# Attention and routed experts: cast loads, 64-row diagonal products, one copy a pair, 1 MB weight loads

## The chip, the core and the metric

The kernel runs on one NeuronCore of a Trainium2 chip. TensorE (PE) multiplies, VectorE (DVE) and ScalarE (ACT) work on vectors, GpSimd (POOL) works on vectors and issues most of the transfers, SyncE (SP) issues transfers only. The metric is the device time of one execution in microseconds (us); lower is better.

## The reference

```
scores = q @ k^T / 8, for 8 batches x 8 heads, 576 rows of 64
mask:  row block >= column block, blocks of 64 rows
attn   = softmax(scores);  x = attn @ v        -> 4608 rows of 512 (heads side by side)
for e in 0..7:  rows with domain_id == e:  out = relu(x @ w1[e]) @ w2[e]   (512 -> 1024 -> 512)
```

All inputs are float32; the kernel computes in float16 and adds up in float32.

## The kernel before

**Attention** (lines 289 to 471) goes over 32 pairs of heads, four pairs a batch. For pair p it makes: `emit_T`, 36 transposes of q and k as 64x64 tiles into the PSUM tile PT, one half for q and one for k, each copied by DVE to QK (L302); `emit_G` 0 to 2, the scores of key chunks against later queries, and in the last of them 12 products of 64x64 for the diagonal blocks (L336), followed on ACT by exps (L315), four a pair: two of 1024 columns, one of 512, and one of 384 that puts the diagonal blocks into ATE; `emit_P` and `emit_Q`, the products with v into the one PSUM tile `po`: 20 of 65 columns (L366), and 5 of 130 columns that do the diagonal blocks of both heads at once (L361), with ATE zero-padded to 128 rows against VE, a copy of v with the heads in separate row halves. A column of ones beside v gives the softmax sums; `emit_Q` ends with a reciprocal and a multiplication on DVE (L382, L383) into the tile x.

The order is written out by hand (`manual_schedule`): each engine runs its instructions in the order of the code. In the round of pair p, PE gets G0(p), T(p+2), G1(p), P(p-1), G2(p), Q(p-1). Sorting the tokens by domain (`routing`, `inverse`) is cut into steps, one a round, mostly DVE work, some with PE products into PT buffers.

**Loads.** q and k are cast from float32 to float16 by the transfer, issued by POOL, 64 partitions each (L71); two buffers hold two batches each. v comes as float32 into `vst` (three buffers), that of batch 0 on SP's queue (L88), the others on POOL's, one load a head (L104, L108); it is then cast to `vS` by POOL (L114), for batch 0 by DVE. `loads(p)` says in which round POOL issues them. The weights of experts 0 and 1 are loaded in rounds 20 and 22, w1 and w2 in four parts each (L120, L123).

**Experts** (lines 477 on). At the end of each batch the tile x goes to x_rows in device memory. When all has landed, POOL gathers the rows of each expert (L484, five blocks of 128), issues the weights of expert 2, and from then on the weights of expert e+3 between the five scatters of expert e (L540). PE transposes the gathered rows (L494) and does `mm1` (L516) and `mm2` (L533).

Of the kernel before, what the change touches and what calls it, by code (L numbers as in the profile page):

```python
# [18 lines left out]
def kernel(  # L19
# [20 lines left out]
    NH = NJ // 2  # L40

# [25 lines left out]
    def load_qk(g0, g1):  # L67
        t, o = divmod(g0, 2 * HP)
        for src, dst in ((q, qh), (k, kh)):
            for i in range(2):  # L70
                nc.gpsimd.dma_start(  # L71
                    out=dst[t % 2][64 * i : 64 * i + 64, o : o + g1 - g0, :],
                    in_=src.rearrange("b (g i) (p j) d -> i p (b g) (j d)", i=2, j=9)[
                        i, :, g0:g1, :])

    load_qk(0, 1)
# [6 lines left out]

    nc.gpsimd.memset(vst[0][:, :, 0, 0:1], 0.0)
    load_qk(1, HP)
    for c in range(5):
        n = min(128, S - 128 * c)
        nc.sync.dma_start(  # L88
            out=vst[0][0:n, c], in_=v[0, :, 128 * c : 128 * c + n, :].rearrange(
                "h p d -> p h d"))  # L90
    load_qk(HP, 2 * HP)
    up = const.tile([128, 128], F16, name="up")
    make_upper_triangular(nc, up[:], 1.0, diag=False)
    iota_i = const.tile([128, 128], I32, name="iota_i")
    nc.gpsimd.iota(out=iota_i[:], pattern=[[1, 128]], base=0, channel_multiplier=0)
# [6 lines left out]
    def load_v(b, h0, h1):  # L102
        for h in range(h0, h1):
            nc.gpsimd.dma_start(  # L104
                out=vst[b % 3][:, 0:4, h, :],
                in_=v[b, h, 0:512, :].rearrange("(c p) d -> p c d", p=128))
        if h1 == H:
            nc.gpsimd.dma_start(  # L108
                out=vst[b % 3][0:64, 4],
                in_=v[b, :, 512:S, :].rearrange("h p d -> p h d"))  # L110

    def cast_v(fn, b):
        for pr, cs in ((128, slice(0, 2)), (128, slice(2, 4)), (64, slice(4, 5))):
            fn(  # L114
                out=vS[b % 3][0:pr, cs, :, 2:130],
                in_=vst[b % 3][0:pr, cs].rearrange(
                    "p c (g i) d -> p c g (i d)", i=2))

    def w1_piece(w1h, w1_e, i):
        nc.gpsimd.dma_start(out=w1h[:, i], in_=w1_e[128 * i : 128 * i + 128, :])  # L120

    def w2_piece(w2h, w2_e, i):
        nc.gpsimd.dma_start(  # L123
            out=w2h[:, 2 * i : 2 * i + 2],
            in_=w2_e[256 * i : 256 * i + 256, :].rearrange("(p r) f -> p r f", r=2))

    def load_w1(pool, bufs, w1_e):
        w1h = pool.tile([128, 4, Fdim], F16, name="w1h", tag="w1h", bufs=bufs)
        return w1h, [lambda i=i: w1_piece(w1h, w1_e, i) for i in range(4)]

    def load_w2(pool, bufs, w2_e):
        w2h = pool.tile([128, 8, DM], F16, name="w2h", tag="w2h", bufs=bufs)
        return w2h, [lambda i=i: w2_piece(w2h, w2_e, i) for i in range(4)]

    def load_weights(pool, bufs, w1_e, w2_e):
        w1h, t1 = load_w1(pool, bufs, w1_e)
        w2h, t2 = load_w2(pool, bufs, w2_e)
        return w1h, w2h, t1 + t2

    load_v(1, 0, H)  # L140


# [9 lines left out]
    for i in range(3):  # L152
        nc.vector.memset(vS[i][:, :, :, 1:131:129], 1.0)
    for i in range(2):
        nc.vector.memset(ATE[i][:, 0:64], 1.0)
        nc.vector.memset(ATE[i][:, 64:832], 0.0)
        nc.vector.memset(VE[i][:], 0.0)
        nc.vector.memset(VE[i][0:64, :, :, 1:2], 1.0)
        nc.vector.memset(VE[i][64:128, :, :, 130:131], 1.0)
    po = aps.tile([128, 2, 512], F32, name="po")  # L160
    nc.vector.memset(po[:, 1, 264:396], 1.0)

    def inverse(sb, pp, tag, pbufs, ncols, base, tok):
# [5 lines left out]
        for hf in range(2):  # L172
# [7 lines left out]
            nc.vector.tensor_scalar(  # L180
                out=Hh[:, 1], in0=Hh[:, 0], scalar1=p_f[:, 0:1], scalar2=None,
                op0=ALU.mult)
            nc.vector.tensor_tensor(
# [9 lines left out]
            ps = pp.tile([128, 512], F32, name=tag, tag=tag, bufs=pbufs)  # L193
# [40 lines left out]
    def routing():  # L234
        for m in range(0, 128, 32):
            nc.vector.tensor_copy(
                out=iota_x[:, m : m + 32],
                in_=iota_i[:, m : m + 32].unsqueeze(2).to_broadcast([128, 32, NH]))
            yield
        nc.vector.tensor_copy(out=iota_h[:], in_=iota_i[:])  # L240
        nc.vector.tensor_copy(out=p_f[:], in_=p_i[:])
        nc.vector.memset(ones_sq[:], 1.0)
        dom_f = asb.tile([128, NJ], F16, name="dom_f")
        nc.vector.tensor_copy(out=dom_f[:], in_=dom_i[:, 0 : 2 * NJ : 2])
        me = asb.tile([128, E, NJ], F16, name="me")
# [8 lines left out]
        ps_t = aps.tile([128, 512], F32, name="PT", tag="PT", bufs=2)  # L254
        ps_r = aps.tile([128, 512], F32, name="PT", tag="PT", bufs=2)
        nc.tensor.matmul(out=ps_t[:, 0:nj], lhsT=ones_sq[:],
                         rhs=me[:].rearrange(fl), start=True, stop=True)
        nc.tensor.matmul(out=ps_r[:, 0:nj], lhsT=up[:],
# [4 lines left out]
            data1=ps_t[:, 0:nj], initial=0.0, op0=ALU.mult, op1=ALU.add)  # L263
        rk = asb.tile([128, E, NJ], F32, name="rk")
        nc.vector.tensor_tensor(out=rk[:].rearrange(fl), in0=inc[:].rearrange(fl),
                                in1=ps_t[:, 0:nj], op=ALU.subtract)
        nc.vector.tensor_tensor(out=rk[:].rearrange(fl), in0=rk[:].rearrange(fl),
                                in1=ps_r[:, 0:nj], op=ALU.add)
        yield
        nc.vector.tensor_scalar(out=cnt[:], in0=inc[:, :, NJ - 1], scalar1=-1.0,  # L270
                                scalar2=None, op0=ALU.add)
        nc.vector.tensor_tensor(out=rk[:].rearrange(fl), in0=rk[:].rearrange(fl),
                                in1=me[:].rearrange(fl), op=ALU.mult)
        rank = asb.tile([128, NJ], F32, name="rank")
# [3 lines left out]
        ri = slot_col(asb, rank[:], dom_f[:], NJ, u_f[:], "t")  # L278
        lo_i = asb.tile([128, NJ], I32, name="lo_i")
# [3 lines left out]
        yield  # L283
        nc.vector.memset(base_f[:], 0.0)
        yield from inverse(asb, aps, "PT", 2, E * NB, base_f[:, 0:1], tok0[:])

    def emit_T(p):
        b = p // HP  # L290
        QK = asb.tile([128, 2, S], F16, name="QK", tag="QK", bufs=3)
        g = p % (2 * HP)
        for s, src in enumerate((qh[b // 2 % 2], kh[b // 2 % 2])):
            PT = aps.tile([128, 9, 64], F16, name="PT", tag="PT", bufs=2)
            for j in range(9):
                for i in range(2):
                    h = slice(64 * i, 64 * i + 64)
                    nc.tensor.transpose(  # L298
                        out=PT[h, j],
                        in_=src[h, g, 64 * j : 64 * j + 64],  # L300
                        identity=identh[h, h])
            nc.vector.tensor_copy(  # L302
                out=QK[:, s].rearrange("p (n j) -> p n j", j=9),
                in_=PT[:].rearrange("p j n -> p n j"))
        return QK
# [11 lines left out]
    def emit_G(g, st):  # L317
# [11 lines left out]
        else:  # L329
            mm_qk(ps[:, :, 0:256], QK, 2)  # L330
            for m in range(6):
                n0 = 128 * min(m, 4)
                c0 = 256 + 64 * (m % 3)
                for i in range(2):
# [5 lines left out]
            st["A3"] = asb.tile([128, 2, 256], F16, name="A3", tag="A3", bufs=2)  # L340
# [17 lines left out]
    def emit_pv(st, w, m):  # L358
        b, hp = divmod(st["p"], HP)
        o = po[:, w // 3, 132 * (w % 3) : 132 * (w % 3) + 132]  # L360
        nc.tensor.matmul(  # L361
            out=o[:, 1:131], lhsT=st["AE"][:, 128 * m : 128 * m + 128],
            rhs=VE[b % 2][:, m, hp, 1:131], start=True, stop=(m == 0))
        for i in range(2):
            for c in range(m):
                nc.tensor.matmul(  # L366
                    out=o[:, 1 + 65 * i : 66 + 65 * i], lhsT=at_block(st, i, c, m),
                    rhs=vS[b % 3][:, c, hp, 1 + 65 * i : 66 + 65 * i],
                    start=False, stop=(i == 1 and c == m - 1))

    def emit_P(st):
        for m in range(1, 4):
            emit_pv(st, m - 1, m)


    def emit_Q(st):
        hp = st["p"] % HP
# [33 lines left out]
    def loads(p):  # L411
# [8 lines left out]
        if p == 4 * B - 12:  # L420
            w1s[0], t1 = load_w1(wsb, 2, moe_w1[0])
            w2s[0], t2 = load_w2(wsb, 2, moe_w2[0])
            for f in t1:
                f()
# [217 lines left out]
```

## Time and profile before

| | us |
|---|---|
| median of 3 runs | 339.78 (337.0 to 343.36) |
| span of the profiled execution | 337.3 |
| TensorE busy, modelled | 274.4 |
| VectorE, ScalarE, GpSimd busy | 154.0, 140.6, 198.6 |

The profiled execution's own time is not listed apart from its span; the three runs lie between 0.3 below and 6.1 above that span. In the view by stretches a row gives the stretch, its length, the busy time of PE, PEld (weight loads of PE), DVE, ACT and POOL with the number of instructions, then the granted clock of PE as a share of full speed, the busy share of the 16 DMA engines (over 1 where packets overlap) and GB/s as written at the destination. In the timeline a row gives start, length, engine, line and operation; in square brackets the idle time before it and what ended it. In the view of groups a row ends with busy time and mean ns of one.

### The profile page before, as it was taken

The numbers are of one execution on the slowest core, as the hardware profiler recorded it, in microseconds if no ns is written. First come the engines' busy times: TensorE is split into PE (matmuls) and PEld (weight loads), VectorE is DVE, ScalarE is ACT, GpSimd is POOL, SyncE is SP. The second block draws the span as 40 slices with busy tenths as digits, with TensorE's granted clock in tenths as the row PEclk, the third lists the DMA queues.
The fourth block names the chain that finished last, engine by engine and source line by source line (L and its number), as shares of the span: only waits on it lengthen the run. The fifth ranks groups of instructions, "written<-read, shape, count | busy, mean of one in ns | idle before, by whom it ended". The sixth has DMA issues, their size and how long they took to land. (4 is left out here: it accounts for less than half of the span.)

```text
span 337.3 us, 8495 instructions
## 1 busy us (share of the span) xinstructions
PE 274.4 (81%) x3622; PEld 179.6 (53%) x3622; DVE 154.0 (46%) x294; ACT 140.6 (42%) x201; POOL 198.6 (59%) x263
## 2 busy tenths in 40 slices
PE   2404968798989999797169999999999999999930
PEld 1303745566656767575146565665656575656510
DVE  6105896997685688674110433223140504142120
ACT  1211955674753889787015042332405060513200
POOL 8657399556848654000278777768778787523230
PEclk9999995978767899989559999999999999999995
DMA  6999968993899759912337999896989999402020
GB/s 97 205 220 196 221 187 167 218 247 112 153 224 225 150 125 188 220 47 72 84 98 138 251 208 233 166 244 151 211 226 199 233 186 261 157 36 103 32 111 1
DMA packets 36279, 55.66 MB, mean 165 GB/s; under 512 B 9646, under 2 KB 22446, under 8 KB 36240
## 3 DMA queue, kind: packets, MB, share of 16 engines
q0 software_dynamic: 25936, 49.17, 68.2%
q1 hardware_dynamic: 9776, 5.81, 6.6%
q8 instruction: 29, 0.48, 0.5%
q10 hardware_dynamic: 528, 0.13, 0.2%
q14 instruction: 10, 0.08, 0.1%
HBM read 67.15 MB, written 15.20 MB: 244 GB/s over the span
## 5 line engine op out<-in xcount | busy, mean ns | idle before, releaser
L315 ACT ACTIVATE A<-ps 128x1024 f16<-128x1024 f32 (+1 forms) x96 | 83.2, 883 | 64.2 <-PE ps L310 51.1
L522 ACT ACTIVATE hT<-ph 128x640 f16<-128x640 f32 (+1 forms) x72 | 46.4, 645 | 110.0 <-PE ph L516 94.2
L533 PE MATMUL po<-w2h,hT 128*128 128x512 f16 x320 | 74.9, 379 | 0.0
L516 PE MATMUL ph<-xT,w1h 128*128 128x320 f16 x512 | 73.7, 304 | 1.1 <-DVE xT L497 1.1
L484 POOL DMA_INDIRECT xg<-x_rows,tok x40 | 40.6, 1014 | 43.6 <-DMA x_rows<-x 31.6
L540 POOL DMA_INDIRECT out_dram<-osb,tok x40 | 40.8, 1019 | 39.0 <-DVE osb L539 23.7
L516 PEld LDWEIGHTS <-w1h 128*128 128x128 f16 x512 | 50.8, 99 | 23.9 <-issue 1.6
L497 DVE COPY xT<-pt 128x512 f16<-128x512 f16 x40 | 16.8, 424 | 98.9 <-PE pt L494 98.9
L104 POOL DMA_DIRECT2D vst<-in_v_dram x56 | 42.3, 766 | 25.1 <-DMA kh<-in_k_dram 17.9
L302 DVE COPY QK<-PT 128x576 f16<-128x576 f16 x64 | 45.4, 748 | 8.7 <-PE PT L298 8.4
L533 PEld LDWEIGHTS <-hT 128*128 128x128 f16 x320 | 29.8, 98 | 29.4
L310 PE MATMUL ps<-QK 64*128 64x512 f16 (+3 forms) x256 | 38.6, 343 | 1.8 <-DVE QK L302 1.0
L366 PE MATMUL po<-vS,A 128*128 128x65 f16 x640 | 38.5, 205 | 0.8 <-issue 0.8
L361 PE MATMUL po<-VE,ATE 128*128 128x130 f16 x160 | 34.2, 239 | 4.8 <-DVE x L383 2.9
L298 PE MATMUL PT<-identh,qh 64*64 64x64 f16 x576 | 17.5, 208 | 24.7 <-DVE QK L302 16.2
L539 DVE COPY osb<-po 128x512 f32<-128x512 f32 x40 | 27.4, 684 | 18.8 <-PE po L533 18.8
L366 PEld LDWEIGHTS <-A 128*128 128x128 f16 x640 | 33.8, 106 | 3.4 <-issue 3.0
L298 PEld LDWEIGHTS <-qh 64*64 64x64 f16 x576 | 14.2, 121 | 33.4 <-issue 24.3
L383 DVE TENSOR_TENSOR x<-po,rc 128x768 f16<-128x768 f32 x32 | 30.6, 957 | 1.1
L114 POOL CAST vS<-vst 128x1024 f16<-128x1024 f32 (+1 forms) x21 | 18.8, 928 | 9.0 <-PE po L366 6.8
L494 PE MATMUL pt<-identh,xg 128*128 128x128 f16 x160 | 15.8, 226 | 9.1 <-DMA xg<-x_rows,tok 9.1
L361 PEld LDWEIGHTS <-ATE 128*128 128x128 f16 x160 | 16.3, 102 | 10.1 <-issue 8.0
(84 smaller groups left out, 207.7 us busy)
## 6 DMA issues: line engine op xcount, KB each, us to landing
w1h<-in_moe_w_dram POOLq DMA_DIRECT2D x32, 256.0 KB, 6.4
w2h<-in_moe_w_dram POOLq DMA_DIRECT2D x32, 256.0 KB, 7.9
vst<-in_v_dram POOLq DMA_DIRECT2D x63, 128.0 KB, 5.6
x_rows<-x SPq DMA_DIRECT2D x7, 512.0 KB, 4.8
qh<-in_q_dram POOLq DMA_DIRECT2D x6, 576.0 KB, 9.0
kh<-in_k_dram POOLq DMA_DIRECT2D x6, 576.0 KB, 13.2
vst<-in_v_dram SPq DMA_DIRECT2D x4, 256.0 KB, 15.6
xg<-x_rows,tok POOLq DMA_INDIRECT x40, 3.7
```

The source lines that it names most:

```text
L104: nc.gpsimd.dma_start(out=vst[b % 3][:, 0:4, h, :], in_=v[b, h, 0:512, :].rearrange("(c p) d -> p c d", p=128))
L298: nc.tensor.transpose(out=PT[h, j], in_=src[h, g, 64 * j : 64 * j + 64], identity=identh[h, h])
L302: nc.vector.tensor_copy(out=QK[:, s].rearrange("p (n j) -> p n j", j=9), in_=PT[:].rearrange("p j n -> p n j"))
L310: nc.tensor.matmul(out=o[:, i], lhsT=QK[h, 1, 128 * c : 128 * c + 128], rhs=QK[h, 0, 64 + 128 * c : S], start=True, stop=True)
L315: nc.scalar.activation(out=o, in_=i, func=AF.Exp, scale=0.125)
L361: nc.tensor.matmul(out=o[:, 1:131], lhsT=st["AE"][:, 128 * m : 128 * m + 128], rhs=VE[b % 2][:, m, hp, 1:131], start=True, stop=(m == 0))
L366: nc.tensor.matmul(out=o[:, 1 + 65 * i : 66 + 65 * i], lhsT=at_block(st, i, c, m), rhs=vS[b % 3][:, c, hp, 1 + 65 * i : 66 + 65 * i], star ...
L484: nc.gpsimd.indirect_dma_start(out=g[:, blk, :], out_offset=None, in_=xd, in_offset=bass.IndirectOffsetOnAxis(ap=tok[:, 1, blk : blk + 1], ...
L516: nc.tensor.matmul(out=ph[:, i, 0:hw], lhsT=w1_cols(w1h, dc, fc), rhs=xT[:, dc, hw * i : hw * i + hw], start=(dc == 0), stop=(dc == 3))
L522: nc.scalar.activation(out=hT[:, fc].rearrange("p (i n) -> p i n", i=2)[:, i0:i1], in_=ph[:, i0:i1, 0:hw], func=AF.Relu)
L533: nc.tensor.matmul(out=po[:], lhsT=hT[:, fc, 128 * blk : 128 * blk + 128], rhs=w2h[:, fc, :], start=(fc == 0), stop=(fc == 7))
L540: nc.gpsimd.indirect_dma_start(out=dst[blk], out_offset=bass.IndirectOffsetOnAxis(ap=tok[:, 0, blk : blk + 1], axis=0), in_=osb[:], in_off ...
```

## The change

- q and k: one load of 128 partitions for each, four buffers of a batch each. v is cast by the transfer straight into vS, one load a key chunk of 128 rows for all heads (1024 pieces of 64 numbers); vst, POOL's casts and the loads on SP go. Loads of batch b+3 are issued in round 4b.
- The diagonal products with v read the exps in A3 directly, as tiles of 64 rows, 10 of 65 columns (`emit_D`); ATE and VE go, and VB holds the odd heads' v in the upper rows. The exps of 512 and 384 columns become one of 896.
- PT is one buffer for q and k together, copied by one instruction. T(p+2) stands at the end of the round: G0(p), G1(p), P(p-1), G2(p), D(p-1), N(p-1), T(p+2).
- The first routing step stands before the first transposes, the second right behind them; iota_x and four products of `inverse` move to POOL; the sums of `routing` use `po`.
- Weights in four loads an expert, not eight. Expert 0's are issued in round 17; those of experts 1 and 2 after the first gathers.

```diff
-    qh = [asb.tile([128, 2 * HP, S], F16, name=f"qh{i}") for i in range(2)]
-    vst = [asb.tile([128, 5, H, D], F32, name=f"vst{i}") for i in range(3)]
-    vS = [asb.tile([128, 5, HP, 132], F16, name=f"vS{i}") for i in range(3)]
-    VE = [asb.tile([128, 5, HP, 132], F16, name=f"VE{i}") for i in range(2)]
-    ATE = [asb.tile([128, 832], F16, name=f"ATE{i}") for i in range(2)]
+    RV = 4
+    qh = [asb.tile([128, HP, S], F16, name=f"qh{i}") for i in range(RV)]
+    vS = [asb.tile([128, 5, H, 80], F16, name=f"vS{i}") for i in range(RV)]
+    VB = [asb.tile([128, 5, HP, 80], F16, name=f"VB{i}") for i in range(2)]
...
+    def load_v_chunks(b, h0, h1, cs):
+        for c in cs:
+            n = min(128, S - 128 * c)
+            nc.gpsimd.dma_start(
+                out=vS[b % RV][0:n, c, h0:h1, 16:80],
+                in_=v[b, h0:h1, 128 * c : 128 * c + n, :].rearrange("h p d -> p h d"))
...
+    def w1_half(w1h, w1_e, i):
         nc.gpsimd.dma_start(
+            out=w1h[:, 2 * i : 2 * i + 2],
+            in_=w1_e[256 * i : 256 * i + 256, :].rearrange("(c p) f -> p c f", p=128))
...
-            PT = aps.tile([128, 9, 64], F16, name="PT", tag="PT", bufs=2)
+        PT = aps.tile([128, 2, 1024], F16, name="PT", tag="PT", bufs=1)
...
-            emit_exp(st["A3"][:], ps[:, :, 0:256])
-            st["AE"] = ATE[st["p"] % 2]
-            emit_exp(
-                st["AE"][:, 64:832].rearrange(
-                    "p (a m z) -> p a m z", a=2, z=128)[:, :, :, 0:64],
-                ps[:, :, 256:448].rearrange("p a (m z) -> p a m z", z=64))
+            st["A3"] = asb.tile([128, 2, 448], F16, name="A3", tag="A3", bufs=2)
+            emit_exp(st["A3"][:], ps[:, :, 0:448])
...
+    def emit_D(st):
+        b, hp = divmod(st["p"], HP)
+        for m in (1, 2, 3, 4, 0):
+            w = (m - 1) % 5
+            for i in range(2):
+                h = slice(64 * i, 64 * i + 64)
+                n0 = 256 + 64 * (m % 3)
+                r0 = 64 if m else 0
                 nc.tensor.matmul(
+                    out=po[r0:128, i, 65 * w : 65 * w + 65],
+                    lhsT=st["A3"][h, m // 3, n0 - 64 + r0 : n0 + 64],
+                    rhs=(VB[b % 2][h, m, hp, 15:80] if i else
+                         vS[b % RV][h, m, 2 * hp, 15:80]),
+                    start=False, stop=(m == 0))
...
+    def emit_VB(b):
+        nc.vector.tensor_copy(
+            out=VB[b % 2][64:128, :, :, 16:80],
+            in_=vS[b % RV][0:64, :, 1::2, 16:80])
...
+        if p + 2 < npair:
+            QKs[p + 2] = emit_T(p + 2)
+        if p < npair and (p == 0 or hp == HP - 1 and b + 1 < B):
+            emit_VB(0 if p == 0 else b + 1)
+        next(rout, None)
+        if hp == 0 and b + 3 < B:
+            prefetch(b + 3)
+        if p == 4 * (B - 4) + 1:
+            for e in range(1):
+                for f in weights(e):
+                    f()
...
-    w1s[2], w2s[2], todo = load_weights(msb, 4, moe_w1[2], moe_w2[2])
-    for f in todo:
-        f()
+    for e in (1, 2):
+        for f in weights(e):
+            f()
```

How the order moves, at three places. On POOL at the start, before (`DMA` is a transfer issued, destination first; `x2` twice in a row):

```order
L71 DMA qh_69<-in_q_dram 64x3x576 x2
L71 DMA kh_71<-in_k_dram 64x3x576 x2
L71 DMA qh_69<-in_q_dram 64x4x576 x2
L71 DMA kh_71<-in_k_dram 64x4x576 x2
...
L104 DMA vst_74<-in_v_dram 128x4x64 x8
L108 DMA vst_74<-in_v_dram 64x8x64
```

and of the change, from the same place:

```order
L73 DMA vS_77<-in_v_dram 128x4x64 x2
L80 DMA vS_77<-in_v_dram 64x8x64
L68 DMA qh_69<-in_q_dram 128x2x576
L68 DMA kh_73<-in_k_dram 128x2x576
L80 DMA vS_77<-in_v_dram 128x6x64 x4
L68 DMA qh_70<-in_q_dram 128x4x576
```

Batch 0's v (vS_77) now stands on POOL's queue ahead of batch 1's q and k (qh_70); before, POOL issued batch 1's q and k (`64x4x576`) beside batch 0's v, which was on SP's queue.

On DVE in the first rounds, before:

```order
L302 COPY QK<-PT 128x576 x4
L114 CAST vS_76<-vst_73 128x8x128 x2
L114 CAST vS_76<-vst_73 64x4x128
L392 COPY VE_79<-vS_76 64x20x64 x2
L302 COPY QK<-PT 128x576 x4
L382 RECIPROCAL rc<-po 128x12
```

and of the change:

```order
L273 COPY QK<-PT 128x1152
L235 TENSOR_TENSOR rk<-inc,po 128x288
L237 TENSOR_TENSOR rk<-rk,po 128x288
L273 COPY QK<-PT 128x1152 x2
L361 COPY VB_81<-vS_77 64x20x64
L240 CAST p_f<-p_i 128x1
```

The copies for the third pair now stand ahead of the first instruction that waits for v (the copy to VB); before, they stood behind the casts of v.

On POOL where the experts begin, before:

```order
L120 DMA w1h<-in_moe_w_dram 128x1024 x4
L123 DMA w2h<-in_moe_w_dram 128x1024 x4
L484 DMA xg<-x_rows,tok_135 128x512 x10
L120 DMA w1h<-in_moe_w_dram 128x1024 x4
L123 DMA w2h<-in_moe_w_dram 128x1024 x4
L484 DMA xg<-x_rows,tok_135 128x512 x5
```

and of the change:

```order
L438 DMA xg<-x_rows,tok_136 128x512 x10
L111 DMA w1h<-in_moe_w_dram 128x2x1024 x2
L116 DMA w2h<-in_moe_w_dram 128x2x1024 x2
L111 DMA w1h<-in_moe_w_dram 128x2x1024 x2
L116 DMA w2h<-in_moe_w_dram 128x2x1024 x2
L438 DMA xg<-x_rows,tok_136 128x512 x5
```

Between the first ten gathers and the next five there now stand the weights of two experts, not of one.

## Rows read from the trace of the kernel before

**Rows 1.** The span in 40 slices: granted clock of PE, busy share of DMA.
```profile
PEclk9999995978767899989559999999999999999995
DMA  6999968993899759912337999896989999402020
```
**Rows 2.** Stretches: all of attention's steady part, then six at half clock, summed.
```profile
30.14:161.80 131.66, 115.94 (x2500) 83.43 (x2499) 98.99 (x178) 88.98 (x123) 70.67 (x97) 0.86 0.80 170
...
50.80:57.60 6.80, 5.47 (x87) 3.73 (x87) 3.60 (x7) 3.03 (x4) 6.80 (x10) 0.50 0.82 160
...
sum 34.00, PE 32.42 PEld 21.48 DVE 18.51 ACT 16.55 POOL 19.39; mean PE 5.40 PEld 3.58 DVE 3.09 ACT 2.76 POOL 3.23
```
**Rows 3.** Timeline of the first 34 us.
```profile
1.39 1.31 POOL L71 DMA_DIRECT2D qh<-in_q_dram  x2 [0.82 <-POOLq L626]
...
4.00 0.12 PEld L298 LDWEIGHTS <-qh 64*64 64x64 f16 x1 [4.00 <-DMA qh<-in_q_dram]
...
27.09 1.19 DVE L114 CAST vS<-vst 128x1024 f16<-128x1024 f32 x2 [9.50 <-DMA vst<-in_v_dram]
...
30.14 0.69 PE L298 MATMUL PT<-identh,qh 64*64 64x64 f16 x18 [12.65 <-DVE QK L302]
...
33.83 0.23 PE L361 MATMUL po<-VE,ATE 128*128 128x130 f16 x1
```
**Rows 4.** Timeline of PE over one round at full clock.
```profile
40.48 0.39 PE L310 MATMUL ps<-QK 64*128 64x512 f16 x2
...
41.48 0.39 PE L310 MATMUL ps<-QK 64*128 64x384 f16 x4
41.86 0.22 PE L361 MATMUL po<-VE,ATE 128*128 128x130 f16 x1
...
42.49 0.28 PE L310 MATMUL ps<-QK 64*128 64x256 f16 x2
...
43.01 0.23 PE L361 MATMUL po<-VE,ATE 128*128 128x130 f16 x1
...
43.48 0.39 PE L310 MATMUL ps<-QK 64*128 64x512 f16 x2
```
**Rows 5.** Timeline of ACT over one round at full clock.
```profile
127.42 0.60 ACT L315 ACTIVATE A<-ps 128x512 f16<-128x512 f32 x1 [0.17 <-PE ps L336]
...
128.28 1.95 ACT L315 ACTIVATE A<-ps 128x1024 f16<-128x1024 f32 x2
130.41 0.60 ACT L315 ACTIVATE A<-ps 128x512 f16<-128x512 f32 x1 [0.18 <-PE ps L336]
```
**Rows 6.** Groups by form: DVE's two largest of a round.
```profile
L302 DVE COPY QK<-PT 128x576 f16<-128x576 f16 x64 | 45.4, 748 | 8.7 <-PE PT L298 8.4
L383 DVE TENSOR_TENSOR x<-po,rc 128x768 f16<-128x768 f32 x32 | 30.6, 957 | 1.1
```
**Rows 7.** DMA queues (packets, MB, share) in 30:35, 4:30, 71:80; then whole span.
```profile
q0 software_dynamic: 923, 1.04, 121.2%
...
q1 hardware_dynamic: 4688, 1.18, 28.8%
...
q0 software_dynamic: 356, 0.95, 39.3%
...
q1 hardware_dynamic: 9776, 5.81, 6.6%
```
**Rows 8.** Timeline where attention ends and the experts begin.
```profile
161.50 0.30 PE L361 MATMUL po<-VE,ATE 128*128 128x130 f16 x1
...
178.20 1.00 POOL L484 DMA_INDIRECT xg<-x_rows,tok  x1 [0.30 <-issue]
179.21 2.25 POOL L120 DMA_DIRECT2D w1h<-in_moe_w_dram  x4
...
195.41 8.86 PE L516 MATMUL ph<-xT,w1h 128*128 128x320 f16 x64
204.11 0.39 PE L494 MATMUL pt<-identh,xg 128*128 128x128 f16 x4
```

More of the change, by code (lines that the diff above doesn't have):

```diff
@@ L100 @@
     iota_x = const.tile([128, 128, NH], F16, name="iota_x")
[L102 to L117, printed above, removed]
@@ L131, in load_w2 @@
[L131 to L140, printed above, removed]
+    nc.gpsimd.tensor_copy(
+        out=iota_x[:], in_=iota_i[:].unsqueeze(2).to_broadcast([128, 128, NH]))
+    load_v_chunks(1, 0, H, range(5))
@@ L143, with load_weights @@
+    def load_weights(w1_e, w2_e):
+        w1h = wsb.tile([128, 4, Fdim], F16, name="w1h", tag="w1h", bufs=NW)
+        w2h = wsb.tile([128, 8, DM], F16, name="w2h", tag="w2h", bufs=NW)
+        return w1h, w2h, [lambda i=i: w1_half(w1h, w1_e, i) for i in range(2)] + [
+            lambda i=i: w2_half(w2h, w2_e, i) for i in range(2)]
     ones_sq = const.tile([128, 128], F16, name="ones_sq")
@@ L151, with inverse @@
     tok0 = const.tile([128, 2, E * NB], I32, name="tok0")
-    for i in range(3):
-        nc.vector.memset(vS[i][:, :, :, 1:131:129], 1.0)
+    po = aps.tile([128, 2, 512], F32, name="po")
+    nc.vector.memset(ones_sq[:], 1.0)
+    for i in range(RV):
+        nc.vector.memset(vS[i][:, :, :, 15:16], 1.0)
     for i in range(2):
[L155 to L166, printed above, removed]
+        nc.vector.memset(VB[i][64:128, :, :, 15:16], 1.0)
+    def inverse(sb, pp, tag, pbufs, ncols, base, tok, eng):
         ub = sb.tile([128, NJ], F16, name="ub", tag="ub")
@@ L234, in routing @@
     def routing():
[L235 to L242, printed above, removed]
         dom_f = asb.tile([128, NJ], F16, name="dom_f")
         nc.vector.tensor_copy(out=dom_f[:], in_=dom_i[:, 0 : 2 * NJ : 2])
+        nc.vector.tensor_copy(out=iota_h[:], in_=iota_i[:])
         me = asb.tile([128, E, NJ], F16, name="me")
@@ L356, in at_block, with emit_P @@
         return st["A2"][:, i, 384:512]
-    def emit_pv(st, w, m):
+    def emit_P(st):
         b, hp = divmod(st["p"], HP)
[L360 to L365, printed above, removed]
-                nc.tensor.matmul(
-                    out=o[:, 1 + 65 * i : 66 + 65 * i], lhsT=at_block(st, i, c, m),
-                    rhs=vS[b % 3][:, c, hp, 1 + 65 * i : 66 + 65 * i],
-                    start=False, stop=(i == 1 and c == m - 1))
@@ L371, in emit_P @@
[L371 to L376, printed above, removed]
-        hp = st["p"] % HP
-        emit_pv(st, 3, 4)
-        emit_pv(st, 4, 0)
-        rc = asb.tile([128, 2, 3, 2], F32, name="rc", tag="rc", bufs=2)
-        pv = po[:, :, 0:396].rearrange("p b (w z) -> p b w z", z=132)
-        nc.vector.reciprocal(out=rc[:], in_=pv[:, :, :, 1:131:129])
+        for m in range(1, 5):
+            for i in range(2):
+                for c in range(m):
+                    nc.tensor.matmul(
+                        out=po[:, i, 65 * m - 65 : 65 * m],
+                        lhsT=at_block(st, i, c, m),
+                        rhs=vS[b % RV][:, c, 2 * hp + i, 15:80],
+                        start=(m == 1), stop=False)
@@ L404, with prefetch, weights @@
     npair = B * HP
+    rout = routing()
+    next(rout)
     QKs = {0: emit_T(0)}
[L406 removed]
+    next(rout)
     w1s, w2s = {}, {}
[L411 to L432 removed]
+    def prefetch(b):
+        load_qk(b, 0, HP)
+        load_v_chunks(b, 0, H, range(5))
+    def weights(e):
+        w1s[e], w2s[e], todo = load_weights(moe_w1[e], moe_w2[e])
+        return todo
     prev = None
```

164 lines of the change are left out of this document (68 added, 96 removed).

## The prediction

> **What bounds the kernel now.** I read the 40 slices first. The DMA line is full in the first eighth and falls to nothing around slice 19, and the clock line has its low digits in the middle and around slice 20 [rows 1]: attention is the disturbed part, the experts behind it run at full clock. So the question is what attention costs and what it would cost undisturbed.
>
> From the first pair's second set of v products (33.83) to the last pair's (161.50) lie 31 rounds in 127.7 us, 4.12 us each [rows 3, 8]. One undisturbed round of PE takes 43.48 - 40.48 = 3.00 us [rows 4], and ACT's round is as long: 130.41 - 127.42 = 2.99, of which it waits 0.18 for PE [rows 5]. So PE sets the round, ACT could do it in 2.81. 31 rounds at 3.00 would be 93 us; 34.7 us are lost. [...]
>
> Ahead of the rounds lies the start: PE idles 12.65 us until 30.14, because DVE's copy of QK is queued behind its cast of batch 0's v, which waited 9.50 us for that load [rows 3].
>
> **The change, part by part.**
>
> *Start.* What is new is that batch 0's v is ahead of batch 1 on one queue. The transfers for batch 0: 1.18 MB of q and k as written, at 1.04 MB in 5 us (first row of [rows 7]) 5.65 us. For v cast in the transfer there is no row; 256 bytes are read and 128 written a piece. Lower bound: it moves as q and k do, 0.59 MB written in 2.8 us. As uncast v on POOL's queue: 39.3% of 9 us for 0.95 MB, so 4.4 us for a batch's 1.18 MB. Upper: as v on SP's queue, 28.8% of 26 us, 7.5 us for one batch (4688 packets, 25.6 ns each on one of 16 engines) [rows 7]. I take 4.4, the row with the same pieces on the same queue. From the first issue at 1.39, 10 us of transfers and the 2.6 us that the first small load took to reach PE (4.00) give 14; issuing is the tighter path: 15 transfers at 0.65 (1.31 for two) [rows 3] and some 2 us of small POOL work end at 13.2, so v lands near 15.5. PE's own chain to the first diagonal products (three sets of transposes and two rounds of scores, at half clock, after a routing step) is about as long; I take 17.5 for that point, which stood at 33.83: **-16.3 us**. Between 15 and, with v at 7.5, 21.
>
> *Rounds.* The v products of a round take 0.63 (41.86 to 42.49) and 0.47 (43.01 to 43.48) us for 5 x 130 + 20 x 65 = 1950 columns [rows 4]. The change makes 30 x 65, 1950 too; its ten 64-row tiles go in pairs on different row halves. [...] Gain at most 0.14 a round, loss perhaps 0.2 for more, smaller instructions: I take 0, with -4 to +6 us over 31 rounds. The merged exp saves at most one start on ACT (the two took 128.28 - 127.42 = 0.86 for 896 columns [rows 5], about 0.96 ns a column, as the long ones do): 0, since ACT has 0.18 to spare. DVE loses one copy start (two of 0.748 become one), a sixth of the 0.957 multiplication [rows 6], and routing work that goes to POOL; DVE is not what a round waits for, so 0 by itself, but it is the cover for routing steps: some 0.4 us a round more room for them. With T(p+2) behind the diagonal products, `po` has transposes and two score sets (about 1.4 us) to be emptied in, against some 1.2 us for the reciprocal and the multiplication of 0.957 [rows 6]; before, it had the same work. 31 rounds stay at 3.00: 93.
>
> *Waits that stay or come.* PT is now one buffer, and `inverse` twice puts 18 products into it directly behind the transposes of a round. PE must wait until DVE has emptied the tile: 1.2 of normalization, then a copy of about 1.5 [rows 6], less some 0.65 of transposes (they and the first scores take 1.00 [rows 4]), 2 us each; behind PE stand then the next round's scores and with them ACT. Two such waits are **+4**, and I let the clock fall after each: a mean stretch of 34.0 / 6 = 5.7 us [rows 2] costs half, so **+5.7**. The rounds' losses of 34.7 become 9.7: **-25.0 us**. Attention ends at 17.5 + 93 + 9.7 = 120.
>
> *Do the loads keep up?* Each batch needs 5.65 + 4.4 us and the store of x beside it: SP's queue has 6.6% of 337.3 = 22.3 us, less 7.5 for v, so 1.85 a batch [rows 7]. Eight batches with six stores behind them are 91.5 us, and from 1.39 with 2.6 to land, the last v is there at 95.5. It is needed at the end of round 27, some 4.5 rounds (13.5 us) before the end: loads alone would let attention end at 109. Against 120 that is 11 us of cover; it is gone if v takes more than 5.8 us a batch. Four buffers let POOL issue a batch three ahead, so buffers do not hold it.
>
> *Experts.* Expert 1's weights were loaded under attention and now come behind the gathers, at the place where 179.21 is in this trace. 2.1 MB as written are 10.1 us at the rate of rows 7, landed near 192; its products start at 195.41 [rows 8]. Expert 2's are there at about 202, and the next five gathers, queued behind them, near 204, when their transposes start (204.11). That is nearly late: between 0 and +4, I take **+1**. The later experts' weights are issued two experts ahead, as before. Fewer, larger loads only save POOL's time, which nothing waits for here: 0. The hand-over itself (last store, gathers) does not change.
>
> **Sum.** -16.3 - 25.0 + 1 = -40.3. Against the profiled span, 337.3 - 40.3 = 297.0. The median of the runs shown is 2.5 above that span, the profiled execution nearer the lowest run, so I put **299** for a median. I call faster what is under 333, slower what is over 346.6 (2%, about what runs of this kernel can tell apart).
>
> **A rule against it.** A packet of 256 bytes on SP's queue cost 25.6 ns, while one of q and k, 1152 bytes written from 2304, cost 121.2% x 5 x 16 / 923 = 105 ns [rows 7]: small pieces cost more than twice as much for a byte read. [...]
>
> **The rivals.**
>
> *Transfers bind attention.* v's pieces cost what they did on SP's queue, 7.5 us a batch. Then loads end at 120.3 and attention at 134, which is 14 us later than forecast: 313, and up to 324 if PE's waits for v also cost clock. For it: the row just told. Against: POOL's own row is 4.4. Chance 0.20.
>
> *The waits stay.* The round keeps its 4.12 us because it is routing on DVE, and the clock after it, that still stop PE. Then only the start is gained: 337.3 - 16.3 + 1 + 2.5 = 324.5. For it: the routing steps are still on DVE, in order with the copies that PE needs. Against: four of `inverse`'s products and iota_x are gone from there, and PE needs no PT buffer for the sums. Chance 0.10.
>
> *Slower.* The same pieces, but dearer than any row: the last v then ends attention. At 161.5, where it ends now, 161.5 - 13.5 - 4 - 11.1 leaves 132.9 us for eight batches, 16.6 each, so v at 11.0 us or 38 ns a piece is the point from which nothing is gained but nothing lost; the 2% are passed at 11.8. At twice the SP price, 15 us, attention ends at 194 and the time is near 373. For it: the cast halves the pieces. Against: uncast pieces on this queue are far from it, and q and k are cast at 414 GB/s read. Chance 0.05 for slower, 0.05 for the neighbourhood where it comes out within 2%.
>
> *Better.* The clock stays up and D's pairs overlap: 17.5 + 31 x 2.86 + 4 = 110, at the floor of the loads: 289; below 285 it takes loads at the lower bound too. Chance of less than 285: 0.05.
>
> **How the numbers follow.** My forecast, 285 to 308, has 0.55; transfers bind 0.20; the waits stay 0.10; slower 0.05, unchanged 0.05, better 0.05. The likeliest is 299. The range 285 to 324 leaves out better, unchanged and slower, and half of the rival where the waits stay: 0.20. Faster: 0.55 + 0.20 + 0.10 + 0.05 = 0.90; within 2%: 0.05; slower: 0.05.
>
> **What would show it.** Of the changed kernel: the first diagonal products near 17.5 and no PE idle time of over 3 us before them; rounds of 3.0 us at full clock; two waits of PE for DVE ahead of the 18 products of `inverse`; the copy to VB on DVE waiting for v only in batch 0; attention's last products near 120; expert 1's first product waiting for no weight. A VB copy that waits for v in every batch shows the transfers binding; half-clock stretches that still sum to over 20 us show that the waits stayed. The prediction is wrong if attention ends after 145, or if PE waits for weights in the experts.

## The result and the profile after

317.0 us is the median after (315.95 to 318.71, four runs), against 341.23 for the kernel before on the same chip: a ratio of 0.938 (95% interval 0.932 to 0.945). Ratios, here and below, are of executions in the faster of the two states that occur; medians are of all. Forecast were 299 us and a gain of 40.3; the gain is 24.2 by the medians and 21.8 by the spans of the profiled executions, 315.5 us and before 337.3.

Four pieces of the span tell where the 21.8 us came from. The start gave 16.0 (the first pair's diagonal products, from the one that waits for the copy of v, at 17.81, before 33.83 [rows 3]), the 31 rounds gave 4.2 (123.43 us from there to the last pair's at 141.24, before 127.67), the hand-over to expert 1 cost 0.8 (34.72 from there to its first product at 175.96, before 33.91 [rows 8]), and all behind it gave 2.3. Forecast were 16.3, 25.0, -1 and 0. So one term failed, that of the rounds: they take 3.98 us on average, before 4.12.

The page's two lines, granted clock and DMA, to be held against [rows 1]; the rounds' low digits are now in slices 6 to 14:

```profile
PEclk9999966968799599996599999999999999999995
DMA  7999999999989802113379999999989999402040
```

Stretches of the kernel after (columns: length, busy us and count of PE, PEld, DVE, ACT, POOL, then clock, DMA share, GB/s): the 31 rounds; the first of four stretches at half clock in them and the sum of the four, the answer to [rows 2]:

```profile
17.81:141.24 123.43, 104.26 (x2619) 77.39 (x2618) 83.04 (x124) 84.21 (x91) 46.25 (x53) 0.89 1.12 150
...
42.35:52.59 10.24, 9.05 (x108) 5.98 (x110) 3.34 (x6) 2.85 (x3) 4.19 (x5) 0.50 1.71 186
...
sum 27.31, PE 25.91 PEld 17.58 DVE 10.44 ACT 12.12 POOL 5.56; mean PE 6.48 PEld 4.39 DVE 2.61 ACT 3.03 POOL 1.39
```

Its timeline (start, duration, engine, line; in brackets the idle time before and what ended it), with the places that answer to [rows 3, 4, 8]:

```profile
17.22 0.54 DVE L361 COPY VB<-vS 64x1280 f16<-64x1280 f16 x1 [1.30 <-DMA vS<-in_v_dram]
...
17.81 0.21 PE L343 MATMUL po<-VB,A 64*64 64x65 f16 x1 [0.33 <-DVE VB L361]
...
43.54 4.14 PE L173 MATMUL inv_ps<-Hh,L 128*128 128x120 f16 x18 [2.25 <-DVE QK L273]
...
47.62 1.03 PE L281 MATMUL ps<-QK 64*128 64x512 f16 x6
...
52.09 0.61 PE L281 MATMUL ps<-QK 64*128 64x512 f16 x2
...
63.91 4.14 PE L173 MATMUL inv_ps<-Hh,L 128*128 128x120 f16 x18 [1.94 <-DVE QK L273]
...
75.71 0.64 PE L281 MATMUL ps<-QK 64*128 64x512 f16 x6
...
78.75 0.62 PE L281 MATMUL ps<-QK 64*128 64x512 f16 x5
81.96 0.21 PE L281 MATMUL ps<-QK 64*128 64x128 f16 x1 [2.58 <-issue]
...
141.24 0.20 PE L343 MATMUL po<-vS,A 64*128 64x65 f16 x1
...
175.96 8.86 PE L470 MATMUL ph<-xT,w1h 128*128 128x320 f16 x64
```

v is there at 17.2 and PE waits 0.33 us for it; a clean round is 78.75 - 75.71 = 3.04 (one at half clock is 52.09 - 47.62 = 4.47); the two waits ahead of the 18 products are there, 2.25 and 1.94; and the 18 products take 4.14 us each time. Then PE stops for 2.58 us in the middle of a set of scores, and the releaser is "issue": the profile shows nothing that it waited for.

What PE waited for in the rounds (us in all, times, longest):

```profile
PE ps L281 <- ACT A L286: 4.4, 20, 0.4
PE inv_ps L173 <- DVE QK L273: 4.2, 2, 2.2
PE ps L281 <- issue: 4.1, 2, 2.6
PE po L329 <- DVE x L354: 3.7, 4, 1.2
PE po L343 <- issue: 2.4, 3, 1.2
PE po L343 <- DVE VB L361: 0.3, 1, 0.3
PE PT L269 <- issue: 0.3, 1, 0.3
```

The first line, 0.2 us in each of 20 rounds, stands in clean rounds too and so within the 3.04. The three lines that end in "issue" are six stops, 6.8 us, at 37.2, 82.0, 87.9, 98.1, 104.0 and 124.6. PE's instructions are numbered from 0 in order of start (two of its sequencer, then weight loads and products); by that the products that end these stops have the numbers 1217, 2753, 3009, 3521, 3777 and 4801: each leaves 193 on division by 256. On DMA queue 8 ("instruction" on the page) 31 packets of 16,384 bytes pass in the span, each 0.9 to 1.5 us, beside 3,782 weight loads and 3,782 products of PE: one packet for some 244 of them. Between 110 and 142 us, where the DMA engines are busy for 0.14 of the time, six of seven such packets start 14 to 67 instructions behind a number that leaves 193 (the seventh 138); ahead of the six stops they start 138 to 256 behind it, the one before the stop at 82.0 at 79.7, when PE already stood. The packets ahead of the stops took 0.89 to 0.98 us, no longer than the others: it is their start that is late. And each stop ends 1.28 to 1.50 us after such a packet has ended.

### The profile page after: what moved, and what is told of

It is laid out like the page before. It is cut to its first block, busy times and chain, and to the rows that moved or that the text cites. A ratio compares the mean times of both kernels' runs of the same rounds, so it can differ in the third digit from the quotient of the medians.

```text
span 315.5 us, 8638 instructions
## 1 busy us (share of the span) xinstructions
PE 265.6 (84%) x3782; PEld 175.2 (56%) x3782; DVE 135.7 (43%) x235; ACT 137.0 (43%) x169; POOL 164.8 (52%) x189
## 5 line engine op out<-in xcount | busy, mean ns | idle before, releaser
L286 ACT ACTIVATE A<-ps 128x1024 f16<-128x1024 f32 (+1 forms) x96 | 89.3, 988 | 48.4 <-PE ps L281 44.1
L80 POOL DMA_DIRECT2D vS<-in_v_dram x40 | 33.6, 872 | 24.5 <-DVE rc L353 11.1
L273 DVE COPY QK<-PT 128x1152 f16<-128x1152 f16 x32 | 43.2, 1350 | 4.2 <-PE PT L269 4.1
L493 DVE COPY osb<-po 128x512 f32<-128x512 f32 x40 | 27.4, 684 | 21.8 <-PE po L487 16.7
L329 PEld LDWEIGHTS <-A 128*128 128x128 f16 x640 | 24.9, 105 | 14.6 <-issue 14.5
L329 PE MATMUL po<-vS,A 128*128 128x65 f16 x640 | 28.5, 205 | 3.7 <-DVE x L354 3.7
L354 DVE TENSOR_TENSOR x<-po,rc 128x640 f16<-128x640 f32 x32 | 26.4, 824 | 1.1
L281 PEld LDWEIGHTS <-QK 64*128 64x128 f16 x256 | 12.7, 100 | 17.3 <-issue 9.6
L448 PEld LDWEIGHTS <-xg 128*128 128x128 f16 x160 | 12.3, 100 | 17.2 <-issue 8.2
L353 DVE RECIPROCAL rc<-po 128x10 f32<-128x10 f32 x32 | 7.1, 222 | 31.4 <-PE po L343 31.4
L343 PE MATMUL po<-vS,A 64*64 64x65 f16 (+1 forms) x160 | 17.3, 206 | 0.0
```

The costliest lines, as they stand in the source:

```text
L80: nc.gpsimd.dma_start(out=vS[b % RV][0:n, c, h0:h1, 16:80], in_=v[b, h0:h1, 128 * c : 128 * c + n, :].rearrange("h p d -> p h d"))
L273: nc.vector.tensor_copy(out=QK[:].rearrange("p s (n j) -> p s n j", j=9), in_=PT[:, :, 0:S].rearrange("p s (j n) -> p s n j", j=9))
L281: nc.tensor.matmul(out=o[:, i], lhsT=QK[h, 1, 128 * c : 128 * c + 128], rhs=QK[h, 0, 64 + 128 * c : S], start=True, stop=True)
L286: nc.scalar.activation(out=o, in_=i, func=AF.Exp, scale=0.125)
L329: nc.tensor.matmul(out=po[:, i, 65 * m - 65 : 65 * m], lhsT=at_block(st, i, c, m), rhs=vS[b % RV][:, c, 2 * hp + i, 15:80], start=(m == 1) ...
L448: nc.tensor.transpose(out=pt[:, dc], in_=g[:, blk, 128 * dc : 128 * dc + 128], identity=identh[:])
```

## The experiments

Theory 1: the 18 products of `inverse` are dear by themselves, as they read L and Hh in steps of 18 elements. Theory 2: PE's own instructions come late while data queues are full. Rivals stand with each run. In this table attention's end is the start of the last pair's last diagonal products, stops are those of over 0.25 us at numbers that leave 193, and "half" is the half-clock stretches that end before attention does; the ratio is to the kernel before on the same chip. The first three columns are of one profiled execution each, and executions of one kernel differ: those without q and k from batch 4 on took 309.3 to 313.8 us.

| run | attention ends | stops, us | half, us | median, us | ratio, interval |
|---|---|---|---|---|---|
| the changed kernel | 141.2 | 6, 6.8 | 27.3 | 317.0 | 0.938, 0.932 to 0.945 |
| products first | 140.3 | 6, 7.6 | 30.7 | 314.8 | 0.919, 0.915 to 0.923 |
| columns side by side | 136.5 | 5, 6.6 | 30.7 | 313.0 | 0.913, 0.910 to 0.917 |
| both of these | 137.1 | 9, 11.3 | 27.3 | 312.3 | 0.912, 0.909 to 0.916 |
| no q, k, v from batch 4 on | 132.1 | 2, 2.4 | 17.1 | 306.7 | 0.896, 0.893 to 0.900 |
| no v from batch 4 on | 137.1 | 5, 6.3 | 23.9 | 314.4 | 0.922, 0.915 to 0.929 |
| no q, k from batch 4 on | 139.6 | 8, 8.9 | 17.1 | 309.8 | 0.916, 0.907 to 0.924 |
| no q, k, v, and both edits | 124.8 | 3, 5.1 | 6.8 | 300.0 | 0.879, 0.873 to 0.885 |
| loads twice | 146.7 | 9, 12.5 | 30.7 | 321.5 | 0.949, 0.940 to 0.958 |
| quarter batches | 143.9 | 5, 6.8 | 30.7 | 321.1 | 0.941, 0.935 to 0.946 |
| quarter batches, both edits | 135.0 | 5, 8.0 | 20.5 | 314.0 | 0.918, 0.912 to 0.925 |
| five buffers, both edits | 144.0 | 7, 8.9 | 27.3 | 319.8 | 0.945, 0.940 to 0.950 |
| five buffers, loads behind | 136.9 | 9, 12.2 | 20.5 | 313.3 | 0.923, 0.917 to 0.928 |

**Products first.**

```diff
+        if p in (7, 11):
+            next(rout, None)
         if p + 2 < npair:
             QKs[p + 2] = emit_T(p + 2)
...
-        next(rout, None)
+        if p not in (7, 11):
+            next(rout, None)
```

> The two sets of 18 products of `inverse` are issued ahead of a round's transposes instead of behind them, so that nobody has filled the one PT buffer just before. In the changed kernel rounds 7 and 11 take 9.44 and 9.59 us, of which PE waits 2.25 and 1.94 for DVE and the 18 products take 4.14 each; the last diagonal products start at 141.4. Theory 1 (three costs side by side: the wait, the products themselves at 230 ns each because their operands are read in steps of 36 bytes, and the clock after the wait): the two waits shrink to some 0.4 each, the products stay at 4.1, rounds 7 and 11 come to 7.4 to 7.9, attention ends at 138 if the clock falls all the same and near 135 if it does not; 309 to 314 us. Rival (the step as predicted: the wait and the fall of the clock are all there is): rounds 7 and 11 come near 5, attention ends near 132; about 307.

The products and the transposes behind them:

```profile
43.80 4.14 PE L173 MATMUL inv_ps<-Hh,L 128*128 128x120 f16 x18
48.32 0.69 PE L269 MATMUL PT<-identh,qh 64*64 64x64 f16 x18 [0.37 <-DVE inv L176]
```

The wait shrank to 0.37 as expected and the products stayed at 4.14. The rival is out: the rounds took 8.99 and 8.11 us, not 5. But theory 1's end (135 to 138) was missed too: the stop at number 1217 was 1.83 us long, up to 39.0, and the clock fell in it, at 38.7, ahead of the products. A wait that the edit does not touch stands in that end as well, with 3.4 us at half clock behind it: PE waited for batch 1's k, as in the next two runs (1.87 and 0.81 us), and not in the trace of the changed kernel.

```profile
24.39 0.47 PE L269 MATMUL PT<-identh,kh 64*64 64x64 f16 x18 [1.55 <-DMA kh<-in_k_dram]
```

**Columns side by side.**

```diff
-            L = sb.tile([128, 128, NH], F16, name="L", tag="L")
-            Hh = sb.tile([128, 3, ncols, NH], F16, name="Hh", tag="Hh")
+            L = sb.tile([128, NH, 128], F16, name="L", tag="L")
+            Hh = sb.tile([128, NH, 3, ncols], F16, name="Hh", tag="Hh")
...
-                nc.tensor.matmul(out=pv, lhsT=L[:, :, j], rhs=Hh[:, :, :, j],
+                nc.tensor.matmul(out=pv, lhsT=L[:, j], rhs=Hh[:, j],
```

The steps that make the two tiles are changed to match.

> L and Hh of `inverse` are laid out with the 128 and 120 columns of one product side by side in place of 18 elements (36 bytes) apart; the order is left as in the changed kernel. Theory 1: the products are slow because of the steps in which they read; they fall from 230 to 120 ns or less, 18 of them from 4.1 to about 2, the two waits stay at about 2, and attention ends at 136 to 138 (141.4 in the changed kernel); 311 to 314 us. Rival (they are slow because they run at half clock after the wait): they stay at 230 ns, attention ends at 141 and the time is that of the changed kernel, 317.

```profile
45.71 1.98 PE L174 MATMUL inv_ps<-Hh,L 128*128 128x120 f16 x18 [1.46 <-DVE QK L274]
...
63.84 1.12 PE L174 MATMUL inv_ps<-Hh,L 128*128 128x120 f16 x18 [2.45 <-DVE QK L274]
```

110 ns a product at half clock (38.0 to 51.7), 62 at full clock, where the steps made it 230 at either: in the changed kernel the first set ran wholly at half clock, the second half and half, and both took 4.14. Theory 1 holds, and end and time are where it had them. Both operands were changed at once, so which of the two costs more is not shown, nor what makes steps of 36 bytes dear: 230 against 62 ns is what the traces have.

**Both edits.**

> Both edits together. Theory 1: the waits and the steps add; rounds 7 and 11 come to 5 to 5.5 us, no half-clock stretch starts in them, attention ends at 131 to 134; 306 to 309 us. Rival (the clock falls in these rounds whatever PE waits for, since routing keeps it from its rounds): the half-clock stretches after rounds 7 and 11 stay and attention ends at 135 or later.

Theory 1's end (131 to 134) did not come; the rival's did (135 or later), but not for its reason: both half-clock stretches near these products (from 38.1 and 58.5) began behind stops, up to 36.96 and 57.65, and ahead of the products. Attention ended no earlier than with the second edit alone. The waits for QK are gone and the transposes wait 0.37 as before, though the first set now waits 1.5 for L. But the stops grew from 6.8 to 11.3 us:

```profile
PE ps L282 <- issue: 5.2, 4, 1.7
PE po L344 <- issue: 3.8, 3, 1.9
PE PT L270 <- issue: 2.3, 2, 2.0
PE inv_ps L174 <- DVE L L165: 1.5, 1, 1.5
```

What `inverse` gave went into stops. That PE, being faster, reaches the next number that leaves 193 earlier, while the loads keep their length, is a guess at the reason; no run tried it apart.

**No q, k, v from batch 4 on.**

```diff
-        if hp == 0 and b + 3 < B:
+        if p == 0:
             prefetch(b + 3)
```

> Left out: q, k and v of batches 4 to 7 are not loaded (their rounds compute with the data of batches 0 to 3). Nothing else is changed; the weights of expert 0 are still loaded in round 17. In the changed kernel PE stops six times, 6.8 us in all, at every instruction whose number is 193 modulo 256, where no semaphore holds it, and the clock falls after the two longest stops (at 82 and 104 us). Theory 2 (PE's own instructions come in pieces of 256 on DMA queue 8 and are late when the data queues are full): the stops at 82 and 88 vanish and with them the half clock at 83.3, attention ends at 135 to 138; the stops during the load of the weights (98 and 104) stay. Rival 1 (the fetch itself is too slow for PE, whatever else moves): the stops stay where they are, attention ends at 140 to 141. Rival 2 (the loads slow PE in other ways too): steady rounds come below 3.0 us.

From 60 us on not one stop is left, and rounds 14 to 29 take 3.04 or 3.05 us each; rival 1 is out, and rival 2 with it. It went further than expected: POOL, free of loads, issued the weights earlier, so that they were in by 73 us and the stops at 98 and 104 went as well. Between 79 and 107 us the 16,384-byte packets start 7 to 55 instructions behind a number that leaves 193; in the changed kernel, between 79 and 102, they start 83 to 256 behind it. The whole of the 9.2 us is in the rounds.

**Which of them? No v, and no q and k.** In `prefetch`, the one or the other line is made to hold for batch 3 alone.

> Left out: v alone of batches 4 to 7 is not loaded; q and k are. Without any of the three the stops of PE at every 256th instruction after 60 us were gone and attention ended at 132.1 instead of 141.2. Theory 2a (the 4608 pieces of 128 bytes that each batch's v is made of hold up the pieces of PE's instructions): the stops after 60 us vanish here too, attention ends at 131 to 134; 305 to 309 us. Theory 2b (any full data queue does it, q and k as well): most stops stay, attention ends at 137 to 141; 312 to 317.

> Left out: q and k alone of batches 4 to 7 are not loaded; v is, in its pieces of 128 bytes. Without v alone, the stops at 85, 91 and 97 us stayed, 3.6 us in all, while q, k and then the weights were loaded. Theory 2b (what counts is that the queue is full, with whatever): v fills some 4 us a batch and stops PE once or twice after 60 us, 1 to 3 us in all; attention ends at 135 to 138; 310 to 314 us. Theory 2a (the small pieces alone): stops as in the changed kernel, 5 us or more after 60 us, attention ends at 139 to 141. Rival (q and k alone): none, 132.

Without v, three stops of 3.6 us stayed between 85 and 97, while q, k and the weights moved, and the end (137.1) is in the range of 2b. Without q and k, five stops of 5.2 us came after 60 us, as 2a said, though its time of 309.8 is near what 2b said (the profiled execution, 313.8, was the longest of five, so its trace shows more than a usual loss). Neither kind alone is the cause; how their shares divide stays open.

**No q, k, v, and both edits.** The two edits to `inverse` with the one on `prefetch`.

> Left out: q, k and v of batches 4 to 7, as before; and both edits to `inverse` are made (columns side by side, products ahead of the transposes). Theory: these are the two causes of what the rounds still lose, and they add: 132.1 less some 11 us that rounds 7, 8, 11 and 12 lost; attention ends at 119 to 125, where the prediction had it (120); 293 to 300 us. Rival (there is a third loss, the clock falls by itself in these rounds): attention ends at 127 or later, 302 or more.

```profile
17.35:124.79 107.44, 92.79 (x2631) 71.50 (x2630) 84.46 (x125) 84.06 (x91) 24.82 (x26) 0.97 0.68 107
```

Attention ends at 124.8, with the clock at 0.97 over the rounds and only 6.8 us at half clock. Of the 21 us by which the forecast end of 120 was missed, the two causes hold 16.4. What is left has names as well: three stops of 5.1 us, two of them while batch 3 was loaded and one under the weights.

**Loads twice.** The converse, in the stretch that had hardly a transfer (0.14 of the DMA engines' time between 111 and 140):

```diff
             prefetch(b + 3)
+        if p in (21, 25):
+            prefetch(b - 1)
```

> Added: in rounds 21 and 25, where the changed kernel has hardly a transfer left (from 110 us on), batches 4 and 5 are loaded a second time into their own finished buffers; nobody reads them again. Theory 2 (PE's instructions come late while data queues are full): the 256th instructions of 110 to 135 us, of which one now stops PE for 0.32 us, stop it three or more times, 3 us or more in all, and the clock falls once or twice more; attention ends at 145 to 152 (141.2); 320 to 328 us. Rival (the earlier stops came from where in the program they lie, not from transfers): no new stop, attention ends at 141 to 142; 317.

```profile
114.79 0.19 PE L269 MATMUL PT<-identh,kh 64*64 64x64 f16 x1 [1.27 <-issue]
121.26 0.19 PE L343 MATMUL po<-VB,A 64*64 64x65 f16 x1 [0.19 <-issue]
128.00 0.22 PE L269 MATMUL PT<-identh,kh 64*64 64x64 f16 x3 [2.63 <-issue]
```

Three stops, 4.1 us, where there was one of 0.32; the clock fell behind two of them (115.6 to 119.0 and 129.3 to 136.1). Attention ended 5.5 us later, though round 23 began 1.7 us earlier (110.41, in the changed kernel 112.10): from there on 7.2 us were lost. Theory 2 holds from this side too. Whole times leave it open, as the two ratios' intervals overlap (0.940 to 0.958, and 0.932 to 0.945); the trace decides here.

**Quarter batches, alone and with both edits.** Loads per round in place of per batch:

```diff
-        if hp == 0 and b + 3 < B:
-            prefetch(b + 3)
+        if b + 2 < B:
+            load_qk(b + 2, hp, hp + 1)
+            load_v_chunks(b + 2, 0, H, (hp, 4) if hp == 3 else (hp,))
```

> Nothing left out: each round loads a quarter of the batch two ahead (q and k of one pair, one or two chunks of v) instead of a whole batch at once three ahead, and each of the four loads of expert 0's weights has a round of its own from round 24. The same bytes in smaller portions: some 1.8 MB a 12.2 us. Theory 2c (PE's instructions are late when a whole batch stands in the queue): the stops shrink to a third, attention ends at 133 to 137 (141.2 in the changed kernel); 309 to 313 us. Rival (it is the number of pieces that counts, however they come): the stops are as long, only elsewhere; attention ends at 140 or later; 316 or more. A second one: a load comes too late and PE waits for q, k or v.

> The portions of a quarter batch together with both edits to `inverse`. Theory: the gains add; attention ends at 124 to 130; 301 to 306 us. Rival (the stops stay and take what `inverse` gives, as in the run with both edits alone): attention ends at 135 or later, 311 or more.

The rival won both times. Alone, the stops came to the same 6.8 us, later in the span (82 to 127), and the loads lasted longer (to 118.3 us, in the changed kernel to 108.8). With both edits the stops were 8.0 us, not 11.3, and attention ended some 2 us earlier than with the edits alone, but 2.8 us were lost behind it. So smaller portions of the same bytes did not bring the time down.

**Five buffers, twice.** Batches loaded four ahead; then the same with batch 4 issued behind the first POOL steps of `inverse`, batches 5 and 6 in round 9, batch 7 and the weights in round 13.

```diff
-    RV = 4
+    RV = 5
...
-        if hp == 0 and b + 3 < B:
-            prefetch(b + 3)
-        if p == 4 * (B - 4) + 1:
+        for bb in {0: (3,), 5: (4,), 9: (5, 6), 13: (7,)}.get(p, ()):
+            prefetch(bb)
+        if p == 13:
```

> Nothing left out: both edits to `inverse` (iota_x, which nothing reads then, is gone) and five buffers for q, k and v in place of four, each batch loaded four ahead. The last v and the weights then wait for no buffer, so that the transfers end near 95 us and not at 108. Theory 2: fewer of PE's 256th instructions fall under a full queue, two or three stops fewer than with both edits alone (nine, 11.3 us); attention ends at 130 to 135 (137.1 there); 305 to 310 us. Rival (earlier loads only move the stops to an earlier place, as the portions did): attention ends at 136 to 139; 311 to 314.

> Five buffers as before, but batch 4 is issued in round 5 behind the steps of `inverse` on POOL (in the run before, 18 products waited 11.4 us for such a step that POOL had behind batch 4's loads), batches 5 and 6 in round 9, batch 7 and the weights of expert 0 in round 13: no load waits for a buffer of a late round. Theory 2: without that wait the run before would end attention near 130; the transfers end near 97 us as there (108 in the changed kernel), so two or three stops fewer than with both edits alone; attention ends at 130 to 135, 305 to 310 us. Rival (stops only move earlier and take as much): 136 to 139, 311 to 314.

The first missed by a wait that no theory had:

```profile
42.59 0.74 POOL L68 DMA_DIRECT2D kh<-in_k_dram  x1 [3.42 <-DMA qh<-in_q_dram]
45.39 1.76 POOL L80 DMA_DIRECT2D vS<-in_v_dram  x2 [2.06 <-DMA kh<-in_k_dram]
...
49.94 2.13 POOL L154 TENSOR_SCALAR Hh<-Hh,p_f 128x720 f16<-128x720 f16 x1
52.01 1.41 POOL L157 TENSOR_TENSOR Hh<-Hh,iota_h 128x720 f16<-128x720 f16 x1
53.35 0.85 POOL L68 DMA_DIRECT2D qh<-in_q_dram  x1
53.48 0.76 PE L171 MATMUL inv_ps<-Hh,L 128*128 128x120 f16 x6 [11.43 <-POOL Hh L157]
```

POOL's waits between these issues ended as earlier loads landed (14.2 us in all between 17 and 60), and the step that makes Hh stood behind batch 4's loads: the products waited 11.4 us. The second had no such wait, but nine stops took 12.2 us, and end and time are the rival's. It does not show what an earlier end of the transfers would do, as they ended at 102.8 us, with both edits alone at 104.5. Of the versions that compute everything, both edits alone has the lowest time, though the columns alone are as fast within the intervals: 312.3 us, 0.912 of the kernel before, and 0.972 of the changed kernel (0.9123 / 0.9382; with both intervals some 0.965 to 0.980).

## Why the prediction was wrong, step by step

- **The start** was right: 17.81 for a forecast 17.5. v landed at 17.2, 1.7 later than worked out, and PE's own chain was as long.
- **v on POOL's queue** was right in size, and so the rivals about transfers and about the slower side fell. Between 20 and 25 us 4,167 of v's packets passed, so 4,608 take 5.5, and 4.0 less the time of the q and k among them (0.30 MB), by [rows 7]. The copy to VB waited for v once, in batch 0. One packet of 128 bytes took 32 ns, where 256 bytes took 25.6 [rows 7]; the packets of these 5 us add up to 2.05 times the 16 engines' time, so that some two were under way on an engine at once. So a packet of half the bytes was no shorter. But the pieces did not come to bind the rounds by their rate. The last of v passed before 100 us (forecast 95.5).
- **The round** of 3.00 is 3.04, 1.2 us over 31 rounds; the 64-row products and the merged exps cost about what was said. No run shows the 0.14 a round that the prediction put as the most to be gained by the 64-row products: a clean round came out 0.04 longer. That PE alone sets it does not hold any more: PE waits 0.20 us for ACT in a clean round (the line of 4.4 us above).
- **The two waits** of 2 us are 2.25 and 1.94.
- **"The rounds' losses of 34.7 become 9.7" failed**; they became 123.43 - 93 = 30.4. Three terms were missing and one was too small. *The 18 products themselves*, twice 4.14 us, entered no sum: the prediction priced PE's wait ahead of them and not the products. They stand in the trace of before with the same length, as the group of line 196:

```profile
L196 PE MATMUL PT<-Hh,L 128*128 128x120 f16 x36 | 8.2, 398 | 0.9 <-DVE QK L302 0.9
```

  *The stops that end in "issue"*, 6.8 us, came to 2.6 before, so even these were there to be read. *PE's wait for DVE's multiplication*, 3.7 us (three times behind a routing step, once in the last round), was put at 0 and was 2.9 before:

```profile
PE po L361 <- DVE x L383: 2.9, 7, 1.3
...
PE po L361 <- issue: 1.3, 1, 1.3
...
PE po L366 <- issue: 0.8, 1, 0.8
...
PE PT L298 <- issue: 0.4, 1, 0.4
```

  *The clock* was at half for 27.3 us and not 11.4. That it falls after each wait was the prediction's assumption; here it fell in the first of the two waits (at 42.35) and 2.3 us behind the second (at 66.24), but also behind the longest stop (at 83.3) and in the second longest (at 103.8), and not behind those of 1.16 us (at 37.2) and 0.95 (at 98.1). Some 5.9 us of the 27.3 lie under the slow products, which take as long at either clock, and 1.4 are idle. The rest costs less than the half that the prediction took: a round wholly at half clock lasted 4.47 us (47.62 to 52.09), 1.43 more than a clean one, or 0.32 a us, so 20.0 us cost an estimated 6.4, where 5.7 were forecast. With 4.2 of waits for QK and 1.2 of the round itself, 8.3 + 6.8 + 3.7 + 6.4 + 4.2 + 1.2 = 30.6 stand against 30.4. That is closer than the terms are: it leaves out the first round, 1.1 us over a clean one (64-row products of 0.24 us, as at half clock, not 0.19), and the last two, which lack work (2.77 and 2.43 us).
- **The rival "the waits stay"** (324.5) came nearer than the forecast, 7.5 us off and not 18, with rounds of 3.98 us for its 4.12, and its sign came true, half clock of over 20 us in all. Its reason did not: routing on DVE costs PE some 2.5 us now, and what took its place is other work and other waits. The sign for a wrong prediction, attention ending after 145, did not come, though the term of the rounds was wrong.
- **The range**, 285 to 324, holds the 317.0 by luck: the part above 308 was there for transfers that bind (313) and for half of the waits that stay (324.5), and from 17 us to attention's end PE waited for a load only once, 0.33 us through the copy to VB.
- **The experts** were right: +0.8 for +1, and no product of theirs waited for weights. The 2.3 us gained behind expert 1 were not foreseen, and no run here looked into them.

## What to carry to other kernels

Ask of every idle time of a bounding engine whether its releaser is a semaphore; where it is "issue", count instructions, and look whether the stops keep a fixed distance (here multiples of 256). Price the work that stands behind a wait, not the wait alone, and first from its own row of before. When a kernel's loads are made to run under its fastest matmuls, the gain of either can be taken back by such stops, as that of the two edits was here (stops of 11.3 us for 6.8): without q, k and v from batch 4 on, 2.4 us were left, or 5.1 with both edits; smaller portions (6.8, or 8.0) and earlier issues (8.9 and 12.2) did not bring the time down.

## What the runs showed of the hardware

On the queue that the page calls "instruction", 31 packets of 16,384 bytes passed in the changed kernel and 29 in the one before, beside 7,564 and 7,244 weight loads and products of PE: one for some 244 and 250. The stops of the changed kernel lie multiples of 256 instructions apart, at numbers that leave 193, as do the three that end in "issue" in the trace of before (3521, 4289 and 4545). That PE's instructions come in these packets, 256 in each, is inferred from these counts. In rounds of 172 instructions every 3.04 us, with packets that add up to 1.26 times the DMA engines' time (74 to 110 us), PE stood up to 2.58 us for one. In the thirteen traces of the table all 79 stops end 1.20 to 1.59 us after the end of such a packet, and in the changed kernel the latest packet has the longest stop: started 256 instructions behind a number that leaves 193 it stands ahead of 2.58 us, one that started 138 behind ahead of 0.32. In the changed kernel the six stops, 0.28 to 2.58 us, lie between 37 and 125 us; behind them none of over 0.25 stands in the rest of the span. Unexplained is that the stop at number 3777 lasts 1.52 us, to the hundredth, in six of the thirteen traces. What holds the packet back, no run shows.
